# Convolution stem with its gradients on one core: other queues and another order for the first loads, the element loads and two tiny stores, and one affine pass on another engine

## The chip, the cores and the metric

The kernel runs on one core of one Trainium2 chip. The metric is the device time of one execution in microseconds (us); the engines are TensorE (PE in the rows, its weight loads PEld), VectorE (DVE), ScalarE (ACT), GpSimd (POOL) and SyncE (SP). SP, ACT and POOL issue DMAs; "SPq" is time of SP's instruction queue. The core has 16 DMA engines, and the rows give what share of them was busy.

## The reference, cut to what matters

The forward pass is a strided convolution, a normalization over time for each batch and channel, and a gelu. The kernel returns the output and the gradients of x, w, gamma and beta.

```python
B, T, D, K, s = 2, 16000, 256, 31, 2          # bfloat16
L = (T - K) // s + 1                          # 7985
h = sum(einsum('blc,cd->bld', x[:, i:i + s*L:s, :], w[i]) for i in range(K))
mu = h.sum(1) / L;  var = ((h - mu)**2).sum(1) / L
out = gelu((h - mu) / sqrt(var + 1e-5) * gamma + beta)      # tanh form
outputs: out, and vjp(grad_out) for x, w, gamma, beta
```

dgamma and dbeta are 256 numbers each.

## The kernel before

Three stages run one behind the other on PE: `forward` (matmuls on L372; 2 batches b, 4 chunks c of positions, 3 branches A, B, C of a fast convolution that trades matmuls for additions on DVE), `input_grad` (matmuls on L816; again 2 x 4 chunks, in two halves and 3 branches) and `weight_grad` (matmuls on L1035; nine combinations n = 0 to 8).

Beside PE's matmuls the other engines do this:

- `x_load` brings x of a chunk transposed into one buffer XT (`turn`, L248, issued by SP; a chunk's load can begin when PE and DVE have read the one before). The first chunk comes in eight pieces, of which 3 and 1 are needed first. `load_w` brings 31 weight planes in 16 DMAs, in turns on ACT's and POOL's queue. `f_first` then builds sums of x (L340) and differences of weights (L330) on DVE, and PE begins.
- `w2_part` turns the weights a second time for the input gradient (SP), forms differences (DVE), and stores them to scratch `vl` (POOL).
- `gelu_batch` works one batch off in 16 units (`gelu_unit`, L635 to L669): load h from scratch `hd`, two activations y and y2 (L642, L644), a product z, two sigmoids, products on DVE, a store of dy to scratch `dyd`, and two sums. Batch 0 runs beside the forward pass of batch 1, batch 1 beside the input gradient of batch 0. The buffers h, y, y2, z, s come in sets, three for batch 0 and two for batch 1.
- `elem_finalize` forms dgamma, dbeta and three coefficients, and for batch 1 stores dgamma and dbeta from tile `dgb` (two DMAs of 0.5 KB on POOL, each of 256 elements of two bytes, L707).
- `e_load` loads dy and h of a chunk (eight DMAs on POOL), `e_comp` makes dh of them: an affine pass over h on ACT (L736), a scaling of dy on DVE (L738), and their sum on DVE (L740). `dn_turn` turns dh by 16 transposes on SP and stores it to `dnd`; `d2_piece` loads pieces of it (SP), forms differences on DVE (L946) and stores them to `d2d` (POOL); `weight_grad` reads those.

The order on each engine is not that of the code. Every operation goes through `add`, and `Plan.order` (L98) simulates the engines with costs for each operation, takes among the operations that are ready the one that is due first, and writes all instructions out in the order of their simulated starts. PE's order is fixed; due times of the others follow from PE's position and a slack (`plan.slack`, with PACE for the gelu units). On the chip each engine works its list off in order: an instruction that has to wait holds up all behind it on its engine.

Of the kernel before, what the change touches and what calls it, by code (L numbers as in the profile page):

```python
# [9 lines left out]
FP32 = mybir.dt.float32  # L10
# [27 lines left out]
class Plan:  # L38
# [3 lines left out]
    def __init__(self, tc):  # L42
        self.tc = tc
        self.ops = []
        self.lastw = {}
        self.readers = {}
        self.pe = 0.0
        self.slack = 40.0

# [22 lines left out]
    def add(self, eng, dur, outs, ins, fn, dma=None, slack=None):  # L72
# [21 lines left out]
        self.ops.append(dict(eng=eng, dur=dur, fn=fn, preds=preds, dma=dma, at=self.pe,  # L94
# [3 lines left out]
    def order(self):  # L98
# [72 lines left out]
def conv_stem_kernel(  # L171
# [16 lines left out]
    P = 128  # L188
# [31 lines left out]
    kb = cpool.tile([P, 1], FP32, name="kb")  # L220
# [61 lines left out]
    add("DVE", 0.1, [kb[:]], [], lambda: nc.vector.memset(kb[:], 2.0 * GELU_C))  # L282
# [5 lines left out]
    def x_load(b, c):  # L288
# [4 lines left out]
        if b == 0 and c == 0:  # L293
            for k in (3, 1):
# [3 lines left out]
            for k in (0, 2):  # L298
                for e in range(2):
                    j = 4 * e + k  # L300
                    turn(flat[:, 4 * j:4 * j + 4, 0:nr], src[:, 512 * j:512 * j + 512], nr * 1024)
# [6 lines left out]
    def load_w():  # L308
        zero(W[C_][:, C_, :, 3, 1, :], 512)
        qi = 0  # L310
        for sl, r2 in ((A, 0), (C_, 1)):
            for br, r1 in ((A, 0), (C_, 1)):
                for ch in range(2):
                    i0 = 4 * r2 + 2 * r1
                    for par in range(2):
                        nq = 4 if i0 + par + 24 < K else 3
                        load(W[br][:, sl, ch, 0:nq, par, :],
                             w[i0 + par:i0 + par + 8 * (nq - 1) + 1:8, ch * P:(ch + 1) * P, :].rearrange("q p d -> p q d"),
                             65536 * nq, 512, ("ACT", "POOL")[qi % 2])
                        qi += 1  # L320
# [281 lines left out]
    def gelu_batch(b, base, nset, ngt, noo, base0, pace):  # L602

        sets = [[sb(base + 10240 * s + 2048 * j, 4, HM) for j in range(5)] for s in range(nset)]
        gts = [sb(base + 10240 * nset + 4352 * j, 4, 2, XM) for j in range(ngt)]
        oos = [sb(base + 10240 * nset + 4352 * ngt + 4096 * j, 8, D) for j in range(noo)]
        n = 0
        for c in range(NCK):
            off = 0 if c < 3 else 10
            for e in range(2):  # L610
# [15 lines left out]
                for dh in range(2):  # L626
                    plan.slack = base0 + n * pace
                    gelu_unit(b, c, e, dh, sets[n % nset], gt[:, :, dh, off:off + HM], oo)
# [5 lines left out]
    def gelu_unit(b, c, e, dh, tiles, go, oo):  # L634
# [4 lines left out]
        load(h, hv, 262144, 512, "POOL")  # L639
# [43 lines left out]
    def elem_finalize(b):  # L683
# [15 lines left out]
        else:  # L699
            for i, t in enumerate((dgam, S_dy)):  # L700
                tiny([dgb16[:, i, :]], [dgb_acc[:], t],
                     lambda i=i, t=t: tt(out=dgb16[:, i, :], in0=dgb_acc[:, i, :], in1=t, op=ALU.add))
                out = (out_3, out_4)[i]

                def put(i=i, out=out):
                    with nc.allow_non_contiguous_dma(reason="tiny dgamma/dbeta store"):
                        return nc.gpsimd.dma_start(out=out.rearrange("(dh p) -> p dh", p=P), in_=dgb16[:, i, :])  # L707
                add("POOL", 1.0, [], [dgb16[:, i, :]], put, dma=0.1, slack=plan.slack + 100.0)
# [8 lines left out]


    def e_load(b, c):
        et = ET[(4 * b + c) % 3]  # L720
        for t, d in ((et, dy_d[b][c]), (HE, h_d[b][c])):
            v = d[:].rearrange("p (d k e f) -> p d k e f", d=2, k=4, e=2)
            for dh in range(2):
                load(t[:, dh, 0:3, :, 2:258].rearrange("p k j f -> p (k j) f"),
                     v[:, dh, 1:4].rearrange("p k e f -> p (k e) f"), 6 * 65536, 512, "POOL")
            load(t[:, :, 3, 0, 2:258], v[:, :, 0, 1, :], 2 * 65536, 512, "POOL")
# [508 lines left out]
```

## Time and profile before

| what | us |
|---|---|
| median of 3 runs | 1392.07 (1389.69 to 1400.87) |
| the profiled execution's own time | 1405.98 |
| its span, first to last instruction | 1404.2 |
| PE busy in the span | 1271.2 |
| PE's first matmul starts at | 35.84 |

The rows below come from the profiled execution. It is 13.91 us longer than the median, so sums made against it have to be carried over to the median. In a row of the timeline the numbers are start and duration, `x8` is how many instructions are merged, and the bracket is the engine's idle time before them with what ended it. The wait of an engine is always put down to the last event that it waited for.

### The profile page before, as it was taken

How to read it: one execution, taken by the hardware profiler on the slowest of the kernel's cores; microseconds unless marked ns; L12 is line 12 of the kernel's file. 1: busy time of each engine (PE TensorE's matmuls, PEld its weight loads, DVE VectorE, ACT ScalarE, POOL GpSimd, SP SyncE). 2: the span in 40 equal slices, each digit the busy share in tenths (PEclk: the TensorE clock that was granted, in tenths of full speed). 3: DMA queues.
4: the chain of work that ended last, by engine and by line, in shares of the span. 5: the costliest groups of instructions: out<-in, count | busy, mean ns of one | idle time of the engine just before them, and what ended most of it. 6: DMA issues, size and time to landing. Idle time of an engine off the chain costs nothing.

```text
span 1404.2 us, 19142 instructions
## 1 busy us (share of the span) xinstructions
PE 1271.2 (91%) x7725; PEld 770.2 (55%) x7794; DVE 869.4 (62%) x1094; ACT 504.0 (36%) x674; POOL 268.3 (19%) x397
## 2 busy tenths in 40 slices
PE   0998999999997979888982997999999999989998
PEld 0675778977775954334430443444455555555554
DVE  1954343389987568778862864356645686765462
ACT  0021312278666358668750342422321111112100
POOL 2122100012222323233331351023200000011011
PEclk9999999999999999998996998999999999999999
DMA  9999504348497979897999998569748499886510
GB/s 192 194 177 159 144 1 95 65 113 193 128 146 144 310 236 157 223 240 210 202 182 124 261 265 134 152 207 307 242 147 272 144 286 305 287 269 220 162 60 27
DMA packets 286808, 259.32 MB, mean 185 GB/s; under 512 B 195560, under 2 KB 258248, under 8 KB 280496
## 3 DMA queue, kind: packets, MB, share of 16 engines
q1 hardware_dynamic: 252464, 145.52, 45.7%
q0 software_dynamic: 30032, 110.48, 26.6%
q10 hardware_dynamic: 4224, 2.10, 0.8%
q8 instruction: 61, 1.00, 0.3%
q14 instruction: 27, 0.22, 0.1%
HBM read 128.32 MB, written 83.31 MB: 151 GB/s over the span
## 4 chain that ended last, share of the span: by engine, by line
PE 52%; DMA 22%; DVE 8%; SPq 7%; issue 6%; ACT 3%; POOL 2%; POOLq 0%; DVEq 0%; ACTq 0%
PE ps L372 22%; PE ps L1035 21%; PE ps L816 10%; SPq L248 7%; DMA arena<-in_x_dram 5%; DMA arena<-arena 4%; DMA d2d<-arena 3%; DMA arena<-in_grad_out_dram 3%; DMA arena<-dnd 2%; DVE arena L656 2%; DMA arena<-dyd 1%; DMA dnd<-arena 1%; DMA arena<-hd 1%; DVE arena L946 1%; DVE arena L998 1%
## 5 line engine op out<-in xcount | busy, mean ns | idle before, releaser
L816 PE MATMUL ps<-arena 128*128 128x512 bf16 (+1 forms) x2069 | 465.2, 385 | 65.9 <-DVE ps L428 36.9
L372 PE MATMUL ps<-arena 128*128 128x256 bf16 (+3 forms) x3584 | 460.9, 291 | 53.2 <-DVE arena L340 35.8
L372 PEld LDWEIGHTS <-arena 128*128 128x128 bf16 x3584 | 352.9, 98 | 156.0 <-issue 30.3
L816 PEld LDWEIGHTS <-arena 128*128 128x128 bf16 x2112 | 210.7, 100 | 320.0 <-issue 88.5
L1035 PE MATMUL ps<-arena 128*128 128x512 bf16 (+1 forms) x1990 | 344.7, 333 | 1.8 <-DVE ps L428 0.4
L436 ACT ACTIVATE arena<-ps 128x1024 f32<-128x1024 f32 (+1 forms) x139 | 141.7, 1020 | 490.4 <-PE ps L816 206.4
L1035 PEld LDWEIGHTS <-arena 128*128 128x128 bf16 x2016 | 198.4, 98 | 150.3 <-issue 7.8
L340 DVE TENSOR_TENSOR arena<-arena 128x1087 bf16<-128x1087 bf16 (+3 forms) x150 | 134.8, 933 | 150.4 <-PE ps L372 100.2
L243 POOL DMA_DIRECT2D out_dram<-arena x81 | 58.1, 720 | 436.6 <-DVE arena L1067 327.2
L656 DVE TENSOR_TENSOR arena<-arena 128x1024 bf16<-128x1024 bf16 x160 | 109.8, 690 | 32.3 <-DMA arena<-in_grad_out_dram 16.9
L998 DVE TENSOR_TENSOR arena<-arena 128x4096 bf16<-128x4096 bf16 x42 | 95.9, 2289 | 32.2 <-DMA arena<-in_x_dram 23.0
L946 DVE TENSOR_TENSOR arena<-arena 128x768 bf16<-128x768 bf16 (+3 forms) x112 | 64.5, 639 | 62.9 <-DMA arena<-dnd 43.6
L775 DVE TENSOR_TENSOR arena<-arena 128x516 bf16<-128x516 bf16 (+3 forms) x152 | 72.6, 524 | 44.0 <-PE ps L816 36.9
L428 DVE TENSOR_TENSOR ps<-ps,arena 128x1024 f32<-128x1024 f32 x68 | 82.5, 1226 | 22.7 <-PE ps L1035 21.9
L452 ACT ACTIVATE arena<-ps 128x512 bf16<-128x512 f32 (+1 forms) x64 | 36.8, 577 | 137.2 <-PE ps L372 128.0
L1112 DVE TENSOR_TENSOR arena<-arena 128x2304 bf16<-128x2304 bf16 x36 | 48.1, 1354 | 37.6 <-PE ps L1035 37.2
L243 POOL DMA_DIRECT2D d2d<-arena x70 | 51.6, 738 | 97.9 <-DVE arena L946 92.2
L243 POOL DMA_DIRECT2D arena<-hd x64 | 49.3, 771 | 58.8 <-DMA arena<-hd 19.1
L243 POOL DMA_DIRECT2D dyd<-arena x32 | 24.4, 764 | 162.1 <-DVE arena L656 162.1
L646 DVE SCALAR_TENSOR_TENSOR arena<-arena 128x1024 bf16<-128x1024 bf16 x32 | 39.0, 1220 | 14.4 <-ACT arena L644 8.4
L642 ACT ACTIVATE arena<-arena,stats 128x1024 bf16<-128x1024 bf16 x32 | 39.4, 1234 | 20.8 <-DMA arena<-arena 14.4
L436 ACT ACTIVATE ps<-ps 128x1024 f32<-128x1024 f32 x31 | 31.2, 1008 | 41.4 <-PE ps L1035 21.7
(82 smaller groups left out, 667.3 us busy)
## 6 DMA issues: line engine op xcount, KB each, us to landing
arena<-in_x_dram SPq DMA_DIRECT2D x52, 1024.0 KB, 7.6
arena<-d2d SPq DMA_DIRECT2D x16, 1216.0 KB, 8.8
out_dram<-arena POOLq DMA_DIRECT2D x14, 1024.0 KB, 6.8
d2d<-arena POOLq DMA_DIRECT2D x30, 384.0 KB, 8.0
arena<-dnd SPq DMA_DIRECT2D x10, 960.0 KB, 8.3
vl<-arena POOLq DMA_DIRECT2D x36, 256.0 KB, 4.7
arena<-vl SPq DMA_DIRECT2D x9, 1024.0 KB, 8.5
hd<-arena POOLq DMA_DIRECT2D x8, 1024.0 KB, 6.4
```

What stands on the lines that cost most here:

```text
L243: add(eng, 1.0 if eng == "POOL" else 0.1, [out], [in_, *srcs], lambda: e.dma_start(out=out, in_=in_), dma=dcost(nbytes, run), slack=slack)
L248: lambda: nc.sync.dma_start_transpose(out=out, in_=in_), dma=dcost(nbytes, 256), slack=slack)
L340: lambda: nc.vector.tensor_tensor(out=o, in0=a, in1=b, op=ALU.add))
L372: yield nc.tensor.matmul(ps[:, dh, cs], lhsT=wt, rhs=mv, start=s0, stop=False, skip_group_check=True)
L428: add("DVE", dve(1024, 1), [out], [a, b], lambda: nc.vector.tensor_tensor(out=out, in0=a, in1=b, op=op))
L436: lambda: nc.scalar.activation(out=out, in_=ps, func=ACT.Copy, scale=scale))
L656: add("DVE", dve(1024), [o], [a, b_], lambda: V.tensor_tensor(out=o, in0=a, in1=b_, op=op))
L775: lambda: nc.vector.tensor_tensor(out=o, in0=a, in1=b, op=ALU.add))
L816: yield nc.tensor.matmul(ps[:, e, 0:wide], lhsT=lt, rhs=mv, start=s0, stop=False, skip_group_check=True)
L946: lambda: nc.vector.tensor_tensor(out=out, in0=a, in1=b_, op=ALU.subtract))
L998: add("DVE", dve(4096), [o], [a, b], lambda: nc.vector.tensor_tensor(out=o, in0=a, in1=b, op=ALU.add))
L1035: yield nc.tensor.matmul(ps[:, s, c0:c1], lhsT=lt, rhs=mv, start=s0, stop=False, skip_group_check=True)
```

## The change

- The two stores of dgamma and dbeta leave `elem_finalize` and are held back (`hold`) until PE stands at combination 8 of `weight_grad`.
- The 16 weight loads go from ACT's and POOL's queue to SP's, between the pieces of x: pieces 3, weights of slot A, pieces 1, weights of slot C, pieces 0 and 2. The first weight difference is formed in halves by channel (`ch`).
- h of the gelu units and all of `e_load` are issued by ACT, no longer by POOL.
- The affine pass of `e_comp` becomes a `tensor_scalar` on DVE.
- The planner is given other costs: a DMA that feeds something counts 1.3 times its transfer and 6 us (before 2.5 us) when due times are made, a DMA that feeds a DMA 4 us more, and issuing costs 0.8 us on POOL, 0.4 on SP, 0.15 on ACT. PACE of batch 0 goes from (40, 10) to (20, 9).
- The gelu buffers are rings of their own: for batch 0 three of h, y, s, two of y2, z, two of the gradient and two of the output (before three sets, two, one); for batch 1 two, one, one and two (before two sets, one, one).

```diff
-            full = o["dur"] + (o["dma"] + 2.5 if o["dma"] is not None else 0.15)
+            full = o["dur"] + (1.3 * o["dma"] + 6.0 if o["dma"] is not None else 0.15)
...
+                else:
+                    w = [i for i in w if ops[i]["hold"] <= nextpe]
...
+                if o["dma"] is not None and ops[s]["dma"] is not None:
+                    r += 4.0
...
-        add(eng, 1.0 if eng == "POOL" else 0.1, [out], [in_, *srcs], lambda: e.dma_start(out=out, in_=in_),
+        add(eng, {"POOL": 0.8, "SP": 0.4, "ACT": 0.15}[eng], [out], [in_, *srcs], lambda: e.dma_start(out=out, in_=in_),
...
+            piece(3)
+            load_w(A)
+            piece(1)
+            load_w(C_)
+            piece(0)
+            piece(2)
...
-            w_sub(W[B_][:, sl], W[C_][:, sl], W[A][:, sl])
+            for ch in range(2):
+                w_sub(W[B_][:, sl, ch], W[C_][:, sl, ch], W[A][:, sl, ch])
...
-        load(h, hv, 262144, 512, "POOL")
+        load(h, hv, 262144, 512, "ACT")
...
-            add("ACT", act(2064, 0.05), [hv], [hv, s5, s6],
-                lambda hv=hv, s5=s5, s6=s6: nc.scalar.activation(out=hv, in_=hv, func=ACT.Identity, bias=s6, scale=s5))
+            add("DVE", dve(2064, 4), [hv], [hv, s5, s6],
+                lambda hv=hv, s5=s5, s6=s6: nc.vector.tensor_scalar(out=hv, in0=hv, scalar1=s5, scalar2=s6,
+                                                                    op0=ALU.mult, op1=ALU.add))
...
+            if n == 8:
+                plan.hold = plan.npe
+                dgb_store()
+                plan.hold = -1
...
-    PACE = ((40.0, 10.0), (40.0, 8.0))
+    RINGS = ((3, 2, 2, 2), (2, 1, 1, 2))
+    PACE = ((20.0, 9.0), (40.0, 8.0))
```

At the start of the program SP's list before reads (x pieces, then the second turn of the weights, then a piece of the gradient and the next chunk of x):

```order
L248 DMA_TRANSPOSE arena<-in_x_dram 128x4x272 x8
L248 DMA_TRANSPOSE arena<-in_w_dram 128x2x512 x8
L248 DMA_TRANSPOSE arena<-in_grad_out_dram 128x8x256
L248 DMA_TRANSPOSE arena<-in_x_dram 128x32x272
L248 DMA_TRANSPOSE arena<-in_grad_out_dram 128x8x256
L248 DMA_TRANSPOSE arena<-in_w_dram 128x2x512 x4
```

and now:

```order
L254 DMA_TRANSPOSE arena<-in_x_dram 128x4x272 x4
L249 DMA arena<-in_w_dram 128x4x256 x14
L249 DMA arena<-in_w_dram 128x3x256 x2
L254 DMA_TRANSPOSE arena<-in_x_dram 128x4x272 x4
L254 DMA_TRANSPOSE arena<-in_w_dram 128x2x512 x8
L254 DMA_TRANSPOSE arena<-in_grad_out_dram 128x8x256 x2
L254 DMA_TRANSPOSE arena<-in_x_dram 128x32x272
```

The planner has put both pieces that are needed first ahead of all weights, and the other four behind them.

On POOL the first of the stores from `dgb` stood between the last store of dy, an output and the stores to `d2d` of batch 0:

```order
L243 DMA dyd_3_75<-arena 128x4x256 [waits DMASW1_49,DVE_49]
L243 DMA out_dram<-arena 128x4096 [waits DMASW2_49,Activation_49]
L707 DMA out_dram<-dgb_86 128x2x1 [waits DMASW3_49,DVE_49]
L243 DMA d2d_78<-arena 128x3x256 [waits DMASW4_49,DVE_49]
L243 DMA d2d_78<-arena 128x3x256 [waits DMASW5_49,DVE_49]
L243 DMA d2d_78<-arena 128x2x768 [waits DMASW6_49,DMAHW5_49,DVE_49,Pool_49]
```

and now both stand near the end of POOL's list, ahead of the last nine stores of the weight gradient:

```order
L249 DMA out_dram<-arena 128x2x256 [waits DMASW0_49]
L731 DMA out_dram<-dgb_86 128x2x1 [waits DMASW1_49]
L731 DMA out_dram<-dgb_86 128x2x1 [waits DMASW2_49]
L249 DMA out_dram<-arena 128x2x256 [waits DMASW3_49,DVE_49]
L249 DMA out_dram<-arena 128x2x256 [waits DMASW4_49]
```

On ACT, in the input gradient of batch 0 beside the gelu of batch 1, these stood in a row before (L642, L644, L648, L650, L666 are the unit's activations, L436 and L843 serve PE's PSUM tiles):

```order
L644 ACTIVATE arena<-arena,stats 128x1024
L666 ACTIVATE arena,esum_95<-arena 128x1024
L436 ACTIVATE arena<-ps_105 128x2x512
L436 ACTIVATE ps_102<-ps_103 128x1024
L644 ACTIVATE arena<-arena,stats 128x1024
L843 ACTIVATE ps_105<-ps_105 128x512
L642 ACTIVATE arena<-arena,stats 128x1024
```

and now, with DMA issues among them and y2 of a unit (L659) always behind the sum of the unit before (L681):

```order
L657 ACTIVATE arena<-arena,stats 128x1024
L681 ACTIVATE arena,esum_95<-arena 128x1024
L659 ACTIVATE arena<-arena,stats 128x1024
L249 DMA arena<-hd_1_65 128x4x256
L860 ACTIVATE ps_101<-ps_101 128x512
L444 ACTIVATE arena<-ps_102 128x2x512
```

An element load that waits for its buffer now stands ahead of activations that empty or seed PE's PSUM tiles.

## Rows read from the trace of the kernel before

**Rows 1.** The page, busy time, share of the span and instructions of each engine.
```profile
PE 1271.2 (91%) x7725; PEld 770.2 (55%) x7794; DVE 869.4 (62%) x1094; ACT 504.0 (36%) x674; POOL 268.3 (19%) x397
```
**Rows 2.** Windows: stretch, length, busy PE PEld DVE ACT POOL, granted clock, DMA share, GB/s.
```profile
36.00:130.00 94.00, 88.36 (x644) 63.30 (x643) 58.20 (x61) 16.45 (x33) 16.71 (x24) 0.99 0.99 170
...
500.00:720.00 220.00, 194.72 (x911) 93.99 (x928) 175.84 (x274) 162.13 (x192) 69.59 (x106) 0.94 0.89 214
720.00:775.00 55.00, 26.07 (x102) 11.00 (x103) 19.81 (x36) 10.10 (x10) 13.08 (x21) 0.75 0.98 123
775.00:945.00 170.00, 159.07 (x722) 72.61 (x734) 92.86 (x144) 61.01 (x63) 44.48 (x71) 0.97 0.80 200
...
1045.00:1404.00 359.00, 345.26 (x2027) 201.90 (x2051) 214.98 (x159) 47.88 (x55) 23.09 (x32) 0.99 0.63 206
```
**Rows 3.** Waits of PE: engine, line, released by, us in total, times, longest.
```profile
PE ps L816 <- DVE ps L428: 36.9, 5, 16.8
```
**Rows 4.** Timeline of the first 45 us.
```profile
34.50 1.93 DVE L340 TENSOR_TENSOR arena<-arena 128x2176 bf16<-128x2176 bf16 x2 [5.74 <-DMA arena<-in_x_dram]
35.84 9.52 PE L372 MATMUL ps<-arena 128*128 128x512 bf16 x50 [35.84 <-DVE arena L340]
```
**Rows 5.** The chain that ended last, 0 to 135 us: start, us, what.
```profile
8.01 13.27 SPq L248
...
90.00 35.18 DMA arena<-in_x_dram
```
**Rows 6.** The tile in_x_dram, 0 to 40 us: issue times, and time to landing.
```profile
L248 SPq DMA_TRANSPOSE arena<-in_x_dram x8: 1307/2532/13272, 0.7 to 30.8; - x8
...
DMA to landing us min/median/max: 3.6/7.6/21.9
```
**Rows 7.** DMA from 29 to 36 us, the whole stretch.
```profile
DMA packets 6299, 1.70 MB, mean 243 GB/s; under 512 B 5787, under 2 KB 6299, under 8 KB 6299
```
**Rows 8.** DMA from 720 to 772 us: GB/s in 40 equal slices; issues, median us to landing.
```profile
GB/s 9 343 365 284 161 12 55 58 18 12 42 21 18 12 18 33 12 21 133 418 384 366 327 249 72 12 74 3 28 22 18 84 60 72 154 193 103 93 98 203
...
out_dram<-dgb POOLq DMA_DIRECT2D x2, 0.5 KB, 24.9
```
**Rows 9.** Timeline from 718 to 776 us.
```profile
721.37 0.71 POOL L707 DMA_DIRECT2D out_dram<-dgb  x1
...
743.71 0.73 POOL L707 DMA_DIRECT2D out_dram<-dgb  x1 [15.26 <-DMA out_dram<-dgb]
747.17 3.03 DVE L946 TENSOR_TENSOR arena<-arena 128x1792 bf16<-128x1792 bf16 x4 [17.44 <-DMA arena<-dnd]
...
751.39 7.07 PE L816 MATMUL ps<-arena 128*128 128x512 bf16 x20 [16.81 <-DVE ps L428]
...
770.48 5.85 PE L816 MATMUL ps<-arena 128*128 128x512 bf16 x18 [12.02 <-DVE ps L428]
```
**Rows 10.** Timeline of POOL from 1355 us to the end.
```profile
1358.23 1.45 POOL L243 DMA_DIRECT2D out_dram<-arena  x2 [4.19 <-DVE arena L1067]
1365.14 1.45 POOL L243 DMA_DIRECT2D out_dram<-arena  x2 [5.46 <-DVE arena L1067]
...
1399.74 0.73 POOL L243 DMA_DIRECT2D out_dram<-arena  x1 [1.51 <-DVE arena L1067]
```
**Rows 11.** The lines L736 and L738: duration in ns min/median/max.
```profile
L736 ACT ACTIVATE arena<-arena,stats x16: 2091/2097/2107, 497.8 to 881.1; 128x2064 bf16<-128x2064 bf16 x16
...
L738 DVE TENSOR_SCALAR arena<-arena,stats x16: 749/752/876, 491.5 to 870.1; 128x2064 bf16<-128x2064 bf16 x16
```
**Rows 12.** Groups of POOL: busy us, mean ns, idle before, what ended it.
```profile
L243 POOL DMA_DIRECT2D arena<-hd x64 | 49.3, 771 | 58.8 <-DMA arena<-hd 19.1 <-DVE esum L668 11.8 <-issue 11.8
...
L243 POOL DMA_DIRECT2D arena<-dyd x32 | 24.9, 778 | 23.6 <-DMA arena<-dyd 7.2 <-DMA arena<-arena 6.2 <-issue 5.6
```
**Rows 13.** Waits from 840 to 862 us.
```profile
ACT arena L736 <- DMA arena<-hd: 13.7, 1, 13.7
...
PE ps L816 <- ACT ps L843: 9.3, 1, 9.3
```

More of the change, by code (lines that the diff above doesn't have):

```diff
@@ L48, in __init__ @@
         self.slack = 40.0
+        self.hold = -1
+        self.npe = 0
     def cells(self, ap):
@@ L93, in add @@
             self.pe += dur
-        self.ops.append(dict(eng=eng, dur=dur, fn=fn, preds=preds, dma=dma, at=self.pe,
+            self.npe += 1
+        self.ops.append(dict(eng=eng, dur=dur, fn=fn, preds=preds, dma=dma, at=self.pe, hold=-1 if eng == "PE" else self.hold,
                              slack=self.slack if slack is None else slack))
@@ L293, in x_load, with piece @@
         if b == 0 and c == 0:
-            for k in (3, 1):
+            def piece(k):
                 for e in range(2):
@@ L306, in x_load, with load_w, load_gb @@
         return xt
[L308 to L311, printed above, removed]
-            for br, r1 in ((A, 0), (C_, 1)):
[L313 to L320, printed above, removed]
+    def load_w(sl):
+        r2 = 0 if sl == A else 1
+        if sl == C_:
+            zero(W[C_][:, C_, :, 3, 1, :], 512)
+        for ch in range(2):
+            for br, r1 in ((A, 0), (C_, 1)):
+                i0 = 4 * r2 + 2 * r1
+                for par in range(2):
+                    nq = 4 if i0 + par + 24 < K else 3
+                    load(W[br][:, sl, ch, 0:nq, par, :],
+                         w[i0 + par:i0 + par + 8 * (nq - 1) + 1:8, ch * P:(ch + 1) * P, :].rearrange("q p d -> p q d"),
+                         65536 * nq, 512)
+    def load_gb():
         for i, g in enumerate((gn_gamma, gn_beta)):
@@ L529, in f_first @@
         for sl in (A, C_):
-            w_sub(W[B_][:, sl], W[C_][:, sl], W[A][:, sl])
+            for ch in range(2):
+                w_sub(W[B_][:, sl, ch], W[C_][:, sl, ch], W[A][:, sl, ch])
         ops, third, second = f_sums(xt, B_, 0)
@@ L600, in fwd_stats, with gelu_batch, ring_of @@
         tiny([biy], [beta, tm], lambda: V.tensor_tensor(out=biy, in0=beta, in1=tm, op=ALU.subtract))
[L602 to L606, printed above, removed]
+    def gelu_batch(b, base, nset, nscr, ngt, noo, base0, pace):
+        def ring_of(n, *shape):
+            nonlocal base
+            size = 2 * int(np.prod(shape))
+            base += n * size
+            return [sb(base - (n - j) * size, *shape) for j in range(n)]
+        hs_, ys_, ss_ = (ring_of(nset, 4, HM) for _ in range(3))
+        y2s, zs = (ring_of(nscr, 4, HM) for _ in range(2))
+        gts = ring_of(ngt, 4, 2, XM)
+        oos = ring_of(noo, 8, D)
         n = 0
@@ L716, in elem_finalize, with dgb_store, put @@
         tiny([Cc], [t2, t3], lambda: stt(out=Cc, in0=t2, scalar=-1.0, in1=t3, op0=ALU.mult, op1=ALU.subtract))
+    def dgb_store():
+        for i, out in enumerate((out_3, out_4)):
+            def put(i=i, out=out):
+                with nc.allow_non_contiguous_dma(reason="tiny dgamma/dbeta store"):
+                    return nc.gpsimd.dma_start(out=out.rearrange("(dh p) -> p dh", p=P), in_=dgb16[:, i, :])
+            add("POOL", 1.0, [], [dgb16[:, i, :]], put, dma=0.1)
     def e_load(b, c):
@@ L1165, in conv_stem_kernel @@
             fwd_stats(0)
-            for _ in gelu_batch(0, REG, 3, 2, 1, *PACE[0]):
+            for _ in gelu_batch(0, REG, *RINGS[0], *PACE[0]):
                 pass
```

23 lines of the change are left out of this document (6 added, 17 removed).

## The prediction, made before the changed kernel ran

> **What bounds the kernel now.** The first view is the busy time by engine: PE computes for 1271.2 of 1404.2 us [rows 1], so idle PE is worth at most 133 us, and no other engine comes near: DVE stands at 869.4, ACT at 504.0. The second is the table of windows, to see where PE isn't busy. Its first matmul starts at 35.84 [rows 4]. From 36 to 130 us it idles 94.00 - 88.36 = 5.6 us, from 500 to 720 25.3, from 720 to 775 28.9, from 775 to 945 10.9, from 1045 to 1404 13.7, most of it behind the last matmul [rows 2]. Two places are thus dense in loss: the start, and the 55 us from 720, where the granted clock is 0.75 (it moves between its two levels, 1.2 and 2.4 GHz, there) and the DMA engines are 0.98 busy and yet move only 123 GB/s, against 214 before and 200 behind. The rest of the loss is crumbs. I then asked for each place what the last event ahead of PE was.
>
> **Start.** PE waits for a sum on DVE (L340 at 34.50), and that waits for x [rows 4]. The chain shows why: SP's queue holds 13.27 us on one x piece from 8.01 [rows 5], the pieces take 3.6 to 21.9 us from issue to landing [rows 6], because eight pieces and 16 weight loads from two other queues share the DMA engines. The sum needs four pieces only. After the change those stand ahead of all weights, so PE's first matmul needs four pieces of 272 x 1024 B x 4 (1.11 MB) and the eight weight loads of slot A (2.10 MB together), 3.21 MB; the four pieces of the rest and slot C come behind. At the 243 GB/s of the end of the start [rows 7] that is 13.2 us, after 0.7 us to the first issue [rows 6]. Add 2.3 us for the landing of the last (3.6, the shortest, less 1.3 of issue [rows 6]) and the last half difference of weights: L340 takes 1.93 us for 2 x 2176 elements [rows 4], at the same rate 1.2 us for a half of 2048. Sum 17.4 us, a gain of 18. At the 170 GB/s that the next stretch reaches [rows 2] the load takes 18.9 us and the gain is 13. Part of it can be lost again: PE reaches the second chunk of x earlier, and that load takes 35.18 us from 90.00 [rows 5] in a stretch where the DMA engines are already 0.99 busy [rows 2]; the wait at its end is in the 5.6 us above. If that load lands no earlier than now, all of the gain returns as a wait there. I take -14, bounds 0 and -18; it lies nearer the upper end because SP issues that load as soon as its own list lets it, ahead of less.
>
> **The two small stores.** The first dgb store is issued at 721.37; the second, at 743.71, is held by POOL for 15.26 us until the first has landed [rows 9]. They take 24.9 us in the median for 0.5 KB, and in the row of rates the slices fall from 284 to 161, 12, 55, 58, 18, 12 behind the first, recover to 418 when it lands, and fall again to 72, 12, 74, 3 behind the second [rows 8]. In that time DVE's L946 waits 17.44 us for a load of dnd, PE waits 16.81 us for DVE's seed L428 behind it, and again 12.02 us [rows 9]; these two are most of the 36.9 us that PE waits for L428 in all [rows 3]. Beside the 28.8 us of idle PE, the 20 matmuls behind the first wait take 7.07 us [rows 9], where 50 took 9.52 [rows 4], thus 0.35 instead of 0.19 each: another 3 us or so at the lower clock. Without the stores the stage would idle like its neighbour, 10.9 of 170 us or 6.4% [rows 2], 3.5 us in 55. So 28.8 + 2.6 - 3.5, about 28; I take -27, since later stages could be late for something else, with bounds 0 (the stores are not the cause) and -31.
>
> **Their new place.** Both come ahead of the last nine stores of the weight gradient in POOL's list. In the time of before that place lies between the stores issued from 1358.23 and the pair of 1365.14 [rows 10], so about 44 us before the end. Side by side, they land in 25 to 28 us and nothing is late. One behind the other, as now [rows 9], 2 x 24.9 = 49.8 us: 1359.7 + 49.8 = 1409.5, against an end of 1404.2, and the stores behind them or the buffers that these free could be late by up to 13. I take +2, bounds 0 and +13, nearer to the lower end, because the two now follow each other directly and wait in the list for different semaphores (DMASW1 and DMASW2), so that nothing makes the second wait for the first.
>
> **Affine pass and queues.** ACT loses 16 x 2.097 = 33.6 us and DVE gains 16 x 0.752 = 12.0, by the scaling of the same shape [rows 11]. ACT also gets 96 element loads (64 + 32), at POOL 0.77 us each [rows 12], 74 us at most, less if ACT issues faster, which no row shows. In the densest stretch ACT is busy 162.13 of 220 us [rows 2]; the loads of 16 gelu units and of batch 0's chunks (48) would add 37 and the eight affine passes take 17 away, 182 of 220: it remains under PE. DVE goes from 175.84 to some 182 there. The affine pass for its part held ACT 13.7 us for h, and PE waited 9.3 us for L843 behind it [rows 13]. This wait moves to DVE, where L428 stands behind it, so I don't count it as gained. The question is what the loads wait for: POOL idles 58.8 us ahead of the loads of hd and 23.6 us ahead of those of dyd [rows 12], and these 82 us, as far as they come again, now hold ACT ahead of L843 and L436, which PE needs. Nothing of the trace says how much of it the new order removes. I take 0: POOL loses them too, and its stores to d2d leave earlier. Bounds: -17 (the passes of one batch, if ACT is what is late) and +30 (half of the 82 us, passed on at 9.3/13.7, is 28).
>
> **Planner and rings.** The due times of DMA chains now lie earlier by 3.5 us a DMA, 30% of the transfer and 4 us for each link from DMA to DMA. That bears on the crumbs: 25.3 us of idle PE from 500 to 720 and 10.9 from 775 to 945 [rows 2]. Against it stands that batch 1's units have one y2 and one z, so that y2 of a unit waits for the sum of the unit before, as ACT's new list shows, in the stage where ACT is fullest. I take -6, a sixth of the 36 us; bounds -20 and +15.
>
> **Sum.** -14 - 27 + 2 + 0 - 6 = -45. The profiled execution took 1405.98, so 1361; carried to the median by 1392.07/1405.98 that is 1347.5, called **1348 us**.
>
> **Rivals.**
> First, on the other side: ACT becomes the queue that everybody waits for. All 82 us [rows 12] come again on ACT and reach PE at 9.3 of 13.7 us or more [rows 13], 56 to 82 us. It turns the sum of -45 into a loss from 66 us of such waits on (66 x 0.68 = 45); in full it gives 1417 to 1443, on the median 1403 to 1429, called 1410. For it: ACT's list has the loads in front of PSUM work. Against: 19.1 us alone of the 58.8 ended with a landing of hd [rows 12], and waits of POOL were also waits behind its own stores, which ACT doesn't issue.
> Second, the start gains nothing: SP's queue holds its loads as it held 13.27 us on a piece [rows 5], or the time returns at the second chunk of x. Then -31, and 1361 on the median. The Trainium skill, "DMA: Bandwidth & Descriptors", section "Issuing engines are not separate DMA queues", says that DMAs of all issuing engines run on the same 16 engines and interleave, so that another queue saves issuing time alone. By that the change of queue is worth nothing, and only the order is; the mixed landing times of 3.6 to 21.9 us agree.
> Third, the small stores cost as much at the end, or aren't the cause of the stall: the sum loses 11 to 27 us, and the median becomes 1358 to 1375. For the former speaks that the first store took its time while 0.5 KB was all it moved [rows 8]. The same page, section "Rules for kernel authors", says that a non-contiguous last dimension becomes one descriptor per element, wherever the store stands; by that they need 25 us each at the end too. The row of 24.9 us agrees, and whether they run one behind the other no row tells.
> Fourth, better: the crumbs go to the full bounds of the last two terms, -37 rather than -6, with the rest as it is: -76 and 1317; half way 1332.
>
> **How the numbers follow.** The forecast, within 18 us of 1348, gets 0.64. Start lost 0.08, small stores 0.09, better than 1330 0.09, ACT late 0.10, of which half ends within 14 us of the time before or under it. A measurement of this kernel can tell about 1% from no change, 14 us. Slower by more than that (over 1406) is the upper half of ACT's case: 0.05. Within it (1378 to 1406) is the lower part of ACT's case and the tail of the small stores: 0.09. Faster 0.86. The range takes the forecast, the start and the stores with it, and half of the better case: 1320 to 1386.
>
> **What would show it.** Start: PE's first matmul at 17 to 23 us, and the second chunk of x landing before PE needs it. Stores: the total of PE's waits for L428's seed falls from 36.9 to under 15, the granted clock from 720 on is above 0.95, and dgb's landing at the end is 22 to 28 us after its issue, with nothing late behind. Queues: PE's waits for ACT in the input gradient don't grow by over 10 us. The prediction is wrong if ACT's waits for its own DMAs pass on to PE, or if a stall as long as the old one stands elsewhere in the input gradient.

## The result and the profile after

The changed kernel takes 1344.85 us (median of 4 runs, 1338.74 to 1348.54), the kernel before beside it 1396.47 us (4 runs, 1389.69 to 1403.09): ratio 0.963, 95% interval 0.956 to 0.969, 52 us less. 1348 was predicted. The kernel before was run once more beside the changed one, and its median rose by 4.4 us from the 1392.07 that the prediction started from. Ratios here leave out runs that took over 1.5% more than the fastest of their kernel, so they need not be the quotient of two medians. The profiled execution took 1343.63 us, its span is 1341.9; between the two profiled spans lie 62 us, ten more than between the medians, because that of before was a long one.

The first view is again the page's busy time by engine. PE's 1263.7 are 7.5 us less than in [rows 1] with the same 7725 instructions (the mean granted clock is 0.983 instead of 0.969); the other 55 us are idle time. ACT lost 30 us, POOL 79, DVE gained 12.

```profile
PE 1263.7 (94%) x7725; PEld 766.9 (57%) x7794; DVE 880.9 (66%) x1111; ACT 474.2 (35%) x658; POOL 189.3 (14%) x293
```

The windows of the changed kernel (columns as in [rows 2]) stand at the same times, though every stage begins earlier now. PE is busy for 17.79 us before 36 us, when it had only just started. The stretch from 720 idles 6.4 us (28.9 before), at a clock of 0.91 and with the DMA engines moving 272 GB/s at the share of 0.98 at which they moved 123. From 500 to 720 us ACT is busy for 143.20 us, 19 less than before.

```profile
0.00:36.00 36.00, 17.79 (x110) 11.21 (x111) 19.84 (x24) 1.28 (x1) 6.52 (x14) 1.00 1.07 220
36.00:130.00 94.00, 88.09 (x648) 63.79 (x647) 59.38 (x71) 17.82 (x37) 24.98 (x35) 0.96 1.01 207
...
500.00:720.00 220.00, 199.22 (x890) 89.97 (x907) 184.25 (x277) 143.20 (x163) 40.65 (x68) 0.97 0.95 211
720.00:775.00 55.00, 48.56 (x205) 21.40 (x208) 39.02 (x61) 14.60 (x17) 17.32 (x27) 0.91 0.98 272
```

PE's waits (columns as in [rows 3]) show the two large ones (35.8 and 36.9 us) gone; the largest left is that for the first weights, 18.2. L436 is L428 of before, L444 is L436, L860 is L843. Against 36.9 us for the seed from DVE stand 9.6. ACT costs PE 9.5 + 7.6 + 1.2 = 18.3 us in the input gradient; the same view of before gave 14.1 + 2.1 + 0.2 = 16.4.

```profile
PE ps L380 <- DVE arena L338: 18.2, 2, 15.2
PE ps L833 <- DVE ps L436: 9.6, 6, 3.7
PE ps L833 <- ACT arena L444: 9.5, 3, 3.7
PE ps L833 <- ACT ps L860: 7.6, 3, 3.2
```

The start, in PE's timeline, answers to [rows 4]: the first matmul goes at 15.21 behind the first half difference of weights L338, there is a second wait of 3.00 us for the second half, and then PE works through.

```profile
15.21 0.61 PE L380 MATMUL ps<-arena 128*128 128x512 bf16 x1 [15.21 <-DVE arena L338]
18.82 22.18 PE L380 MATMUL ps<-arena 128*128 128x512 bf16 x143 [3.00 <-DVE arena L338]
```

At the end POOL issues the two stores of dgb (L731) at 1298.03, back to back, 43.9 us before the end. Their landings are not in the records. What the timeline shows is that the stores behind them go out as DVE delivers, and that the last one is issued at 1338.33; between PE's last matmul and the end lie 4.6 us (5.5 before). The DMA view of 1296 to 1342 us (GB/s in 40 slices of 1.15 us) adds that the pair of stores issued 4 us behind them moves at 114 and 111 GB/s, as the pairs ahead of them and later ones do: no stretch of 20 us in which the DMA engines are held is to be seen here.

```profile
1298.03 1.44 POOL L731 DMA_DIRECT2D out_dram<-dgb  x2
1303.49 1.44 POOL L249 DMA_DIRECT2D out_dram<-arena  x2 [4.02 <-DVE arena L1084]
...
1338.33 0.72 POOL L249 DMA_DIRECT2D out_dram<-arena  x1 [1.52 <-DVE arena L1084]
```

```profile
GB/s 0 114 114 1 0 0 0 114 111 0 4 0 0 0 14 0 0 0 0 0 0 0 0 121 107 0 0 0 0 0 121 121 0 0 0 121 107 32 82 0
...
out_dram<-arena POOLq DMA_DIRECT2D x11, 128.0 KB, 2.2
```

By PE's own stages, from the first and last start of each line's matmuls, the 62.3 us divide like this, with the kernels of the experiments beside it:

| kernel | first matmul | forward | input gradient | rest | span |
|---|---|---|---|---|---|
| before | 35.8 | 478.2 | 531.0 | 359.2 | 1404.2 |
| changed | 15.2 | 475.5 | 494.9 | 356.3 | 1341.9 |
| a_dgb_mid | 15.0 | 474.9 | 505.2 | 358.2 | 1353.4 |
| b_dgb_end | 36.6 | 471.7 | 499.2 | 360.2 | 1367.7 |
| b_start | 30.0 | 466.1 | 526.8 | 358.9 | 1381.8 |
| b_start_iss | 14.9 | 479.1 | 532.6 | 356.5 | 1383.1 |
| a_old_start | 35.1 | 466.0 | 491.6 | 360.2 | 1352.9 |
| a_old_costs | 30.9 | 460.7 | 507.8 | 358.6 | 1358.1 |
| a_pool_loads | 15.6 | 469.1 | 503.3 | 358.2 | 1346.3 |
| a_act_affine | 15.8 | 473.6 | 501.9 | 358.9 | 1350.2 |
| b_two | 14.7 | 462.9 | 492.2 | 358.7 | 1328.5 |
| b_dgb_one_run | 34.8 | 473.2 | 496.3 | 360.9 | 1365.2 |
| b_dgb_sp | 32.8 | 467.4 | 522.5 | 357.4 | 1380.1 |
| a_old_rings | 15.3 | 488.5 | 546.3 | 356.1 | 1406.2 |

Each row is one execution. The forward stage scatters by 10 us and more without a visible reason in the edit; the input gradient stands between 491.6 and 507.8 us in the eight kernels in which it isn't held by the stores or the old rings; the rest stays within 5 us.

The sum of the first two columns is when PE reaches the input gradient. In the five kernels with the start of before that is at 500 to 514 us (mean 506), in the six with a first matmul at about 15 us, leaving out a_old_rings, at 478 to 494 (mean 488), and in the two with one at about 30 us, b_start and a_old_costs, at 496 and 492.

### The profile page after: what moved, and what is told of

Read it like the earlier page. It is cut to its first block, busy times and chain, and to the rows that moved or that the text cites. A ratio compares the mean times of both kernels' runs of the same rounds, so it can differ in the third digit from the quotient of the medians.

```text
span 1341.9 us, 19113 instructions
## 1 busy us (share of the span) xinstructions
PE 1263.7 (94%) x7725; PEld 766.9 (57%) x7794; DVE 880.9 (66%) x1111; ACT 474.2 (35%) x658; POOL 189.3 (14%) x293
## 3 DMA queue, kind: packets, MB, share of 16 engines
q0 software_dynamic: 21744, 83.34, 18.3%
## 4 chain that ended last, share of the span: by engine, by line
PE 63%; DMA 15%; DVE 9%; ACT 4%; issue 4%; SPq 3%; ACTq 1%; POOL 0%; POOLq 0%; DVEq 0%
PE ps L380 28%; PE ps L1052 19%; PE ps L833 17%; DMA arena<-in_x_dram 7%; DMA arena<-arena 3%; SPq L254 3%; DVE arena L671 2%; DMA arena<-in_grad_out_dram 2%; DVE arena L1015 1%; DVE ps L436 1%; ACT arena L444 1%; DVE arena L348 1%; DVE arena L963 1%; DMA arena<-dnd 1%; DMA dnd<-arena 1%
## 5 line engine op out<-in xcount | busy, mean ns | idle before, releaser
L380 PE MATMUL ps<-arena 128*128 128x256 bf16 (+3 forms) x3584 | 458.3, 290 | 32.5 <-DVE arena L338 18.2
L444 ACT ACTIVATE arena<-ps 128x1024 f32<-128x1024 f32 (+1 forms) x139 | 141.6, 1019 | 486.3 <-PE ps L833 182.4
L671 DVE TENSOR_TENSOR arena<-arena 128x1024 bf16<-128x1024 bf16 x160 | 109.7, 690 | 30.5 <-DMA arena<-in_grad_out_dram 14.8
L792 DVE TENSOR_TENSOR arena<-arena 128x514 bf16<-128x514 bf16 (+3 forms) x152 | 72.6, 522 | 51.7 <-PE ps L833 51.7
L436 DVE TENSOR_TENSOR ps<-ps,arena 128x1024 f32<-128x1024 f32 x68 | 82.4, 1226 | 32.5 <-PE ps L1052 19.7
L440 DVE SCALAR_TENSOR_TENSOR ps<-ps,arena 128x1024 f32<-128x1024 f32 x24 | 29.5, 1229 | 27.5 <-ACT arena L444 14.9
L444 ACT ACTIVATE ps<-ps 128x1024 f32<-128x1024 f32 x31 | 31.2, 1008 | 44.6 <-PE ps L1052 21.7
```

The lines of the kernel that those rows point to most:

```text
L380: yield nc.tensor.matmul(ps[:, dh, cs], lhsT=wt, rhs=mv, start=s0, stop=False, skip_group_check=True)
L436: add("DVE", dve(1024, 1), [out], [a, b], lambda: nc.vector.tensor_tensor(out=out, in0=a, in1=b, op=op))
L444: lambda: nc.scalar.activation(out=out, in_=ps, func=ACT.Copy, scale=scale))
L671: add("DVE", dve(1024), [o], [a, b_], lambda: V.tensor_tensor(out=o, in0=a, in1=b_, op=op))
L792: lambda: nc.vector.tensor_tensor(out=o, in0=a, in1=b, op=ALU.add))
```

## The experiments

The theory was that of the prediction: the start is worth some 17 us, the two stores some 28, and all the rest about nothing. The rival gave the input gradient's gain to the planner and the queues. An edit can also change the order that the planner writes out for all engines, so most runs differ from their kernel in more than the lines shown; where the order stayed, it is said. Names with a_ start from the changed kernel, with b_ from the kernel before. A difference to the changed kernel is that of two ratios times 1396 us; its uncertainty adds both intervals as squares.

### The small stores

**a_dgb_mid** puts the two stores back into `elem_finalize`:

```diff
-            if n == 8:
-                plan.hold = plan.npe
-                dgb_store()
-                plan.hold = -1
...
+                add("POOL", 1.0, [], [dgb16[:, i, :]], put, dma=0.1, slack=plan.slack + 100.0)
```

> The changed kernel with the two stores of dgamma and dbeta back in elem_finalize. Theory (each of them stalls all DMA for 20 to 28 us and PE behind it): 24 to 31 us slower than the changed kernel, some 1372, with two stretches of under 60 GB/s behind the stores and a PE wait of over 10 us. Rival (the input gradient gained by the new order of the planner, and the stores did little): within 6 us of 1345.

Ratio 0.979 (0.970 to 0.989), 0.0167 or 23 us (plus or minus 16) more than the changed kernel. The DMA view of 685 to 745 us (GB/s in 40 slices, then the issues of dgb with size and median time to landing) shows the two falls; in the profiled execution, the fastest of its four, the stores were issued 4.9 us apart, PE waited 6.7, 2.7 and 11.5 us in that stretch, and the input gradient took 10.3 us more than in the changed kernel's.

```profile
GB/s 271 261 345 27 22 16 16 0 0 33 49 141 152 421 367 172 235 56 7 5 3 21 11 13 4 16 34 233 363 410 452 381 267 99 257 301 301 196 257 371
...
out_dram<-dgb POOLq DMA_DIRECT2D x2, 0.5 KB, 25.9
```

**b_dgb_end** moves the stores to the end in the kernel before, with `hold` and nothing else.

> The kernel before with the two stores alone moved to the end. Theory: 24 to 31 us faster than the kernel before, ratio about 0.980, and PE idle from 720 to 775 us falls from 28.9 to under 8. Rival (order): under 6 us, ratio above 0.995.

Ratio 0.974 (0.965 to 0.984), 36 us less than before, with an interval from 23 to 49. PE idles 3.7 us where it idled 28.9 [rows 2], and the DMA engines move 270 GB/s:

```profile
720.00:775.00 55.00, 51.26 (x230) 23.37 (x234) 47.53 (x85) 20.70 (x20) 23.52 (x36) 0.97 0.98 270
```

**b_dgb_one_run** asks what in the stores it is. Place, queue and number of bytes stay as before, and by the two traces POOL, DVE, ACT and SP do the same work in the same order; the pieces change, and with them the source, one partition of a tile of zeros instead of 128 partitions of dgb.

```diff
-    return nc.gpsimd.dma_start(out=out.rearrange("(dh p) -> p dh", p=P), in_=dgb16[:, i, :])
+    return nc.gpsimd.dma_start(out=out.rearrange("(q n) -> q n", q=1), in_=zt2[0:1, 0:256])
```

> The kernel before with both small stores in their old place and queue, but of 256 zeros in one row instead of dgamma and dbeta (outputs 3 and 4 are left out): 16 runs of 32 bytes where there were 256 of two bytes. Theory (the number of two-byte pieces is what holds the DMA engines): each lands within 8 us, no stretch under 60 GB/s behind it, PE idle from 720 to 775 us under 10, ratio about 0.977 as with the stores at the end. Rival (any small store from POOL's queue in this place drains the queue first and costs its wait): landing over 15 us and a ratio above 0.99.

Ratio 0.979 (0.974 to 0.983), 30 us less, as much as moving them away, and with no other order to explain it. In the same place, 719.59 and 726.62 us, they land after 5.9 us in the median instead of 24.9 [rows 8], and PE runs from 717.83 us for 58.45 us without a wait. The rate still dips, to 95 once and to 54 and 73 once, for a slice or two. A load of dnd by SP beside them lands after 7.0 us in the median, a store to d2d by POOL after 7.9:

```profile
GB/s 202 189 410 284 236 362 337 378 319 319 296 264 273 297 340 404 351 95 273 185 54 73 223 335 464 423 386 392 433 411 319 240 378 392 384 205 113 177 414 243
...
d2d<-arena POOLq DMA_DIRECT2D x12, 384.0 KB, 7.9
arena<-dnd SPq DMA_DIRECT2D x4, 960.0 KB, 7.0
...
out_dram<-zt POOLq DMA_DIRECT2D x2, 0.5 KB, 5.9
```

In the kernel before, the same view as [rows 8] has that load, which SP issues and whose bytes have nothing to do with dgb, landing after 23.9 us:

```profile
arena<-dnd SPq DMA_DIRECT2D x2, 960.0 KB, 23.9
```

```profile
717.83 58.45 PE L816 MATMUL ps<-arena 128*128 128x512 bf16 x269
...
719.59 0.54 POOL L707 DMA_DIRECT2D out_dram<-zt  x1
...
726.62 0.52 POOL L707 DMA_DIRECT2D out_dram<-zt  x1
```

So it is the form of the stores, 256 pieces of two bytes from 128 partitions: 512 bytes in fewer pieces cost next to nothing in the same place. Whether the number of pieces, their size or the number of partitions is what costs wasn't tried apart.

**b_dgb_sp** leaves the pieces and changes the queue:

```diff
-                        return nc.gpsimd.dma_start(out=..., in_=dgb16[:, i, :])
-                add("POOL", 1.0, [], [dgb16[:, i, :]], put, dma=0.1, slack=plan.slack + 100.0)
+                        return nc.sync.dma_start(out=..., in_=dgb16[:, i, :])
+                add("SP", 1.0, [], [dgb16[:, i, :]], put, dma=0.1, slack=plan.slack + 100.0)
```

> The kernel before with the two small stores as they are, in about their old place but issued by SP. Theory (the pieces hold the 16 DMA engines, whoever issues them): 20 to 28 us each again, the same fall of the rate, ratio 0.99 to 1.01. Rival (POOL's queue is what stalls): they land within 10 us and the ratio is about 0.977.

Ratio 0.985 (0.980 to 0.990), between the two expectations. The stall is there: 24.9 us in the median to landing, the rate at 19 GB/s or less over nine slices and low again later, and PE waits 20.8 us at 755 us. POOL's stores to d2d, now on another queue than the small stores, land after 15.0 us in the median instead of 7.9. So other queues' transfers are held whoever issues the small stores. Of the 21 us that it saves, the trace shows 8 in the input gradient: SP issues the second store at 718.30, 5.2 us behind the first, so that the two stalls overlap, where POOL had waited for the first to land [rows 9], and PE has one wait of 20.8 instead of 16.81 and 12.02. The rest lies ahead of it, where the executions scatter.

```profile
GB/s 195 7 202 239 6 0 19 19 6 6 6 6 19 82 381 413 425 400 318 104 61 52 45 38 19 11 57 50 95 58 164 375 422 373 334 329 76 22 316 97
...
d2d<-arena POOLq DMA_DIRECT2D x7, 384.0 KB, 15.0
...
out_dram<-dgb SPq DMA_DIRECT2D x2, 0.5 KB, 24.9
```

### The start

**b_start** takes over the order and the queue of the first loads and the halved weight difference into the kernel before, with the planner's numbers of before. By the traces, ACT's and POOL's lists are those of before without the weight loads, and SP's that of before with them put in.

```diff
+            piece(3)
+            load_w(A)
+            piece(1)
+            load_w(C_)
+            piece(0)
+            piece(2)
...
+            for ch in range(2):
+                w_sub(W[B_][:, sl, ch], W[C_][:, sl, ch], W[A][:, sl, ch])
```

> The kernel before with the start alone changed: pieces 3, weights A, pieces 1, weights C, pieces 0 and 2 on SP, and the difference of weights in halves. Theory: first matmul at 15 to 17 us and a gain of 14 to 18 us, ratio about 0.988. Rival (the gain returns at the second chunk of x, since the other parts of the change keep DMA free there): first matmul as early, but under 8 us in the total, with a longer wait near 130 us.

Ratio 0.995 (0.991 to 0.999), and the first matmul at 29.97 us: neither theory foresaw that. The loads land as in the changed kernel, but DVE waits 17.33 us ahead of its wide sum (L343 here, L340 before):

```profile
8.72 0.73 DVE L343 TENSOR_TENSOR arena<-arena 128x1087 bf16<-128x1087 bf16 x1 [7.12 <-DMA arena<-in_x_dram]
26.78 1.93 DVE L343 TENSOR_TENSOR arena<-arena 128x2176 bf16<-128x2176 bf16 x2 [17.33 <-DMA arena<-in_x_dram]
```

DVE's list shows why. These are its wide sum and its first half difference in b_start, with what they wait for:

```
L343 TENSOR_TENSOR arena<-arena 128x2176 [waits DMAHW5_49,DMAHW6_49,DMAHW3_49,DMAHW0_49]
L333 TENSOR_TENSOR arena<-arena 128x2048 [waits DMAHW7_49,DMAHW4_49]
```

and in the changed kernel:

```
L348 TENSOR_TENSOR arena<-arena 128x2176 [waits DMAHW3_49,DMAHW0_49]
L338 TENSOR_TENSOR arena<-arena 128x2048 [waits DMAHW6_49,DMAHW7_49,DMAHW5_49,DMAHW4_49]
```

In b_start the sum is written out behind the issue of the last x pieces and waits for two of them (DMAHW5, DMAHW6), whose values it doesn't use; in the changed kernel it is written out ahead of them. The planner believed in b_start that SP issues a load in 0.1 us, so that the last pieces came before DVE's sum in its simulated time.

**b_start_iss** changes the issuing costs beside b_start, that of SP (0.1 to 0.4) and by the same line those of POOL (1.0 to 0.8) and ACT (0.1 to 0.15); the order of all engines changes with them:

```diff
-        add(eng, 1.0 if eng == "POOL" else 0.1, [out], [in_, *srcs], ...)
+        add(eng, {"POOL": 0.8, "SP": 0.4, "ACT": 0.15}[eng], [out], [in_, *srcs], ...)
```

> The kernel with the start alone changed, and of the planner's numbers only the issuing costs as in the change (SP 0.4 instead of 0.1 us). By the order, DVE's first wide sum then waits for the two pieces 3 alone (DMAHW3, DMAHW0), where without this it waits for two pieces 0 or 2 as well. Theory (this wait is what kept the first matmul at 30 us there): first matmul at 15 to 17 us and 12 to 18 us less than the kernel before, ratio about 0.989. Rival (the time returns later): first matmul as early and a ratio above 0.994.

The first matmul goes at 14.89 us and the ratio is 0.982 (0.972 to 0.992), 25 us less than before, interval 11 to 39. The theory's 12 to 18 lie in it; the rival's end does not. PE's first waits are those of the changed kernel (below). The early first matmul is thus shown; what it is worth beyond b_start is not. The two ratios are 17 us apart, plus or minus 15, but they come from different sets of executions of the kernel before, and the medians are 1379.65 and 1385.25 us (beside 1393.55 and 1396.39). In the profiled executions PE reaches the input gradient at 496.1 and 494.0 us, 2 us apart where the first matmuls were 15; b_start_iss has a wait of 7.3 us at 115 us, at the second chunk of x, which b_start doesn't have.

```profile
14.89 0.61 PE L375 MATMUL ps<-arena 128*128 128x512 bf16 x1 [14.89 <-DVE arena L333]
18.50 11.77 PE L375 MATMUL ps<-arena 128*128 128x512 bf16 x66 [3.01 <-DVE arena L333]
```

**a_old_start** is the changed kernel with the start of before.

> The changed kernel with the start of before. Theory: 14 to 18 us slower than the changed kernel, about 1361. Rival (one queue matters and order does not, or the gain returns later): under 8 us.

Ratio 0.978 (0.971 to 0.985): 22 us (plus or minus 14) more than the changed kernel, first matmul at 35.15.

**a_old_costs** is the changed kernel with the planner's costs of before.

```diff
-            full = o["dur"] + (1.3 * o["dma"] + 6.0 if o["dma"] is not None else 0.15)
+            full = o["dur"] + (o["dma"] + 2.5 if o["dma"] is not None else 0.15)
...
-                if o["dma"] is not None and ops[s]["dma"] is not None:
-                    r += 4.0
```

and the issuing costs as on the minus side of b_start_iss.

> The changed kernel with all the planner's costs of before (due times, link from DMA to DMA, issuing). Theory: the start is late again at 30 us, 13 to 15 us, and the later stages lose 0 to 8: 1358 to 1368, ratio 0.972 to 0.979. Rival (the new due times carry much of the input gradient's gain): over 25 us slower than the changed kernel.

Ratio 0.972 (0.966 to 0.978), 13 us (plus or minus 13) more. The first matmul is at 30.91, 15.7 us later than in the changed kernel, with the four waits of b_start in DVE's list. In size that would account for all of it, but in the profiled execution it doesn't: the forward stage makes up for 14.8 of the 15.7 us (460.7 instead of 475.5), and the input gradient is 12.9 us longer, with one wait of PE for ACT of 14.1 us:

```profile
PE ps L831 <- ACT arena L442: 18.7, 2, 14.1
```

So the start and the due times aren't told apart by this run.

### Queue, affine pass, rings

**a_pool_loads** (the four `"ACT"` of the element loads back to `"POOL"`):

> The changed kernel with the 96 element loads on POOL again. Theory (as predicted, the queue of these loads is worth about nothing): within 8 us of the changed kernel, PE's waits for ACT no longer than 18 us. Rival A (ACT is held by them): faster by over 8 us. Rival B (POOL's stores are held by them): slower by over 8 us, with DVE waiting for dnd or d2d loads ahead of PE's seeds.

Ratio 0.963 (0.957 to 0.970), the same as the changed kernel's, plus or minus 13 us. In the input gradient PE's waits for ACT fall from 18.3 to 3.7 us, and a new one of 21.6 us for DVE's L792 appears. PE idles 14 us more in the whole span and is busy 9 us less (1254.3).

```profile
PE ps L833 <- DVE arena L792: 21.6, 1, 21.6
...
PE ps L833 <- DVE ps L436: 16.1, 4, 7.5
...
PE ps L833 <- ACT ps L860: 3.5, 2, 3.2
```

**a_act_affine** (the `tensor_scalar` on DVE back to an activation on ACT):

> The changed kernel with the affine pass on ACT again. Theory: within 8 us of the changed kernel, since ACT is 65% busy from 500 to 720 us and gets 16.8 us there. Rival: slower by 10 to 17 us, PE's waits for ACT in the input gradient growing from 18 us by as much.

Ratio 0.964 (0.958 to 0.971), 2 us (plus or minus 13) more. PE's waits for L859, which is L860 of the changed kernel, rise from 7.6 to 27.6 us, as the rival said, but those for DVE and L444 fall from 9.6 + 3.1 + 9.5 = 22.2 to 4.1 + 3.6 + 3.1 = 10.8, together 8.6 us more, no more than the runs scatter.

```profile
PE ps L832 <- ACT ps L859: 27.6, 8, 7.3
...
PE ps L832 <- DVE ps L436: 4.1, 3, 3.0
PE ps L832 <- DVE ps L440: 3.6, 3, 3.0
PE ps L832 <- ACT arena L444: 3.1, 2, 1.7
```

**a_old_rings** gives the changed kernel the buffers and the pace of before:

```diff
-    RINGS = ((3, 2, 2, 2), (2, 1, 1, 2))
-    PACE = ((20.0, 9.0), (40.0, 8.0))
+    RINGS = ((3, 3, 2, 1), (2, 2, 1, 1))
+    PACE = ((40.0, 10.0), (40.0, 8.0))
```

> The changed kernel with the gelu buffers and the pace of before: sets of three and two for all five buffers, one output, PACE (40, 10). Theory (the rings are worth a few us at most): within 8 us of the changed kernel. Rival (one y2 and z in batch 1 cost, as the prediction feared): faster by over 8 us, with fewer waits of PE for ACT in the input gradient.

Ratio 1.012 (1.008 to 1.016): 69 us (plus or minus 11) slower than the changed kernel, and slower than before. Both expectations missed. The waits of PE from 480 to 1050 us show two places:

```profile
PE ps L833 <- ACT ps L860: 31.3, 4, 14.0
PE ps L833 <- POOL arena L258: 23.5, 1, 23.5
PE ps L833 <- ACT ps L444: 21.9, 4, 9.2
PE ps L833 <- DVE ps L436: 14.5, 5, 6.2
```

The 23.5 us stand at the first matmul of the input gradient (at 503.8 us), which waits for dh of the first chunk; the last unit of batch 0 has its first activation at 427.89 us, against 409.67 in the changed kernel. Behind it ACT is the late one, 58.7 us in sum. Its timeline has the units of batch 1 in bursts, two units (four activations) each, most of them 30 to 41 us apart, with waits of PE of 14.0 and 12.7 us at 633 and 704:

```profile
486.63 1.24 ACT L657 ACTIVATE arena<-arena,stats 128x1024 bf16<-128x1024 bf16 x1 [1.17 <-DVE stats L718]
...
490.04 1.23 ACT L659 ACTIVATE arena<-arena,stats 128x1024 bf16<-128x1024 bf16 x1
...
527.26 1.23 ACT L657 ACTIVATE arena<-arena,stats 128x1024 bf16<-128x1024 bf16 x1
...
530.66 1.23 ACT L659 ACTIVATE arena<-arena,stats 128x1024 bf16<-128x1024 bf16 x1
...
556.89 1.24 ACT L657 ACTIVATE arena<-arena,stats 128x1024 bf16<-128x1024 bf16 x1 [6.00 <-DMA arena<-arena]
```

In the changed kernel they go one by one, each y2 (L659) behind a sum (L681):

```profile
501.43 1.22 ACT L657 ACTIVATE arena<-arena,stats 128x1024 bf16<-128x1024 bf16 x1
...
509.56 1.04 ACT L681 ACTIVATE arena<-arena 128x1024 bf16<-128x1024 bf16 x1
...
510.72 1.24 ACT L659 ACTIVATE arena<-arena,stats 128x1024 bf16<-128x1024 bf16 x1
...
515.77 1.23 ACT L657 ACTIVATE arena<-arena,stats 128x1024 bf16<-128x1024 bf16 x1
```

Whether the pace, the single output buffer or the sets are what costs wasn't tried apart, nor which other part of the change they cost it with: b_two, next, has all three as before and is not slow.

**b_two** is the kernel before with two parts of the change and nothing else: the start with its issuing costs, and the stores at the end.

> The kernel before with two parts of the change together and nothing else: the start with its issuing costs, and the two small stores at the end. Theory (these two are nearly the whole gain): 40 to 54 us faster than the kernel before, ratio 0.961 to 0.971. Rival (element loads on ACT, affine pass on DVE, rings and due times carry a good part): ratio above 0.975.

Ratio 0.957 (0.950 to 0.964), 60 us less than before, a little over the theory's 54. The profiled execution is the fastest of five that lie between 1330.28 and 1370.75 us, and their median, 1347.07, is about that of the changed kernel. It beats the kernel before; against the changed kernel (0.956 to 0.969) the intervals overlap, 8 us less with plus or minus 13. Within that, nothing of the gain needs the element loads on ACT, the affine pass on DVE, the rings or the due times.

```profile
0.00:36.00 36.00, 18.28 (x106) 11.14 (x107) 20.39 (x25) 1.28 (x1) 6.67 (x15) 1.00 1.04 229
36.00:130.00 94.00, 93.33 (x706) 68.66 (x705) 60.26 (x72) 21.77 (x46) 28.05 (x39) 1.00 1.02 208
...
720.00:775.00 55.00, 53.41 (x247) 24.57 (x251) 35.09 (x60) 20.90 (x22) 21.78 (x32) 1.00 0.98 236
```

## Why the prediction was right

**The start** was predicted at -14 with bounds 0 and -18. The first matmul came 20.6 us earlier, at 15.21 us and so ahead of the 17 to 23 that were given as the sign, and by 130 us PE had 105.9 us of work behind it instead of 88.5, 17.4 more, though 88.5 is low: four other kernels with the start of before had 92.8 to 94.5. By the start of the input gradient the kernels with the early first matmul are 19 us ahead of those with the start of before, in the mean of one execution each; b_start_iss and a_old_start put 25 and 22 us on it, with intervals that hold -14 too. So the term was too small by some 5 us, if at all. Its sum of 17.4 us for the first matmul counted "the eight weight loads of slot A": a half difference needs the loads of one channel half, four, and so 2.2 MB rather than 3.2, and the other four are the 3.00 us wait behind the first matmul, so that PE works through from 18.8 us, near the sum. What made the term small is the step from 18 to 14, for slower loads and a loss at the second chunk of x: there the changed kernel has one wait of 5.0 us at 112.1 us, as long as the one at 129.5 us before, b_start_iss one of 7.3, and b_two none. The step "the sum needs four pieces only" held for what the sum reads, not for what it waits for: in b_start, with the new order of the loads alone, it waits for the last pieces all the same, and the issuing costs in the planner's table decide that, which the prediction didn't have.

**The two small stores**, -27: the stage gave 28.9 - 6.4 = 22.5 us of idle PE in the window, and the experiments 36, 30 and 23 us. PE's waits for the seed fell to 9.6 us, under the 15 that were the sign; the granted clock is 0.91 from 720 to 775 us, not above the 0.95 that was the other. The mechanism, that the DMA engines' other transfers are held while stores of two-byte pieces go out, is shown by b_dgb_one_run (same place, queue, order and number of bytes, 30 us gained) and b_dgb_sp (another queue, still stalled); why such pieces hold them is not. The 0.19 us a matmul with which the prediction priced the lower clock is that of another line with narrower matmuls; the 269 without a wait in b_dgb_one_run take 58.45 us, 0.22 each, which makes it 2.7 us, and its sum used 2.6. The sentence of the Trainium skill on one descriptor per element ("DMA: Bandwidth & Descriptors", "Rules for kernel authors") agrees with that pair: 256 elements land after 24.9 us, 16 runs of 32 bytes after 5.9.

**Their new place**, +2 with a bound of +13: nothing. The tail is 4.6 us instead of 5.5 [rows 10]. The rival of a late tail did not come. How long the stores take there is not recorded, so the sign of 22 to 28 us stays open; but the stores issued 4 us behind them moved at the usual rate, so a stall as in the input gradient did not come again here, where little else is in flight.

**Affine pass and queues**, 0: a_pool_loads and a_act_affine are 1 and 2 us from the changed kernel, plus or minus 13, with PE's waits moved to other engines. The rival on the other side, ACT held by its own element loads, did not come: PE's waits for ACT went from 16.4 to 18.3 us. The 37 us that the loads were to add to ACT's busy time from 500 to 720 us did not come either: it fell from 162.13 to 143.20, by 19 us, near the 17 of the affine passes.

**Planner and rings**, -6 with bounds -20 and +15: the two terms together are the difference between b_two and the changed kernel, 8 us the other way, plus or minus 13, not to be told from -6 or from zero. But the term was put together wrongly. The issuing costs belong to the start. And the rings and the pace can't be taken out of the sum: undone alone they cost 69 us, far outside the bounds, though the same buffers and pace, with the other parts of before, cost nothing that shows in b_two. The one y2 and z of batch 1, which the prediction counted as a risk, did no harm that shows.

The sum of -45 gave 1348 us, and 1344.85 were measured, 47 us under the median that it started from. That the two large terms carry the gain is shown. That the figure is met within 3 us is partly luck: a -6 for which no run shows anything stands where the start was taken some 5 us too low, and none of the runs could tell 5 us.

## What to carry to other kernels

Before a slow stage is given to its engines, look for a tiny store just ahead of it: half a kilobyte in two-byte pieces took the DMA engines from over 200 GB/s to under 90 for 13 to 17 us each time [rows 8], and fewer and longer pieces or a place where nobody waits for DMA cure it equally. Where a scheduler sets the order, check on the compiled order which transfers an instruction waits for, because a few tenths of a microsecond in a cost table can give it a wait for data that it doesn't use. And before a bundle is credited to its parts, build the one with only the parts that the theory needs: here two parts gave as much as the whole, within 13 us, while one of the others, undone alone, looked worth 69 us.

## What the hardware showed that was not expected

Among other transfers, the two-byte stores hold those of all queues, not of their own alone: issued by SP, the 512 bytes took 24.9 us as from POOL, POOL's own stores landed after 15.0 us instead of 7.9, and the rate over all queues fell to 19 GB/s and less. Two of them issued 5 us apart held PE for 20.8 us, two of which the second waited for the first's landing for 16.81 and 12.02 (b_dgb_sp against [rows 9]). And the busy share of the DMA engines doesn't show it: 0.98 at 123 GB/s [rows 2], 0.98 at 270 in b_dgb_end. Near the end of the changed kernel, with few other transfers beside them, no such fall of the rate is seen behind the same two stores; why the pieces hold other transfers in the one place is open.
